# Relu written into the gated tile itself, a third result tile, and one load moved to GpSimd's queue

## The chip, the cores and the metric

The kernel runs on one core of one Trainium2 chip. The metric is the device time in microseconds of one execution. Every figure of a stage below is from the profile of one execution, whose span (2257.6 us) is a little under the device time. TensorE (PE) multiplies matrices, VectorE (DVE) and ScalarE (ACT) work element by element, GpSimd (POOL) does so too and can issue transfers, and SyncE (SP) issues most transfers.

## What is computed

A causal depthwise convolution with seven softmaxed taps per head runs over x (8 sequences of 4096 tokens, 192 channels). Its result, as 32768 rows of 192, goes through a two-layer net with a hard-swish gate:

```python
h = x @ w_in                       # 192 -> 2048
relu6 = np.clip(h + 3.0, 0.0, 6.0)
g = h * relu6 / 6.0
return (g @ w_out).astype(np.float32)   # 2048 -> 192
```

In the kernel the gate is `min(relu(h/6 + 0.5), 1) * h`, which is the same.

## The kernel before, in words

**Blocks.** The tokens are cut into 32 blocks of 1024 (`NB`), each as two halves of 512 that lie on two halves of the partitions. The order of all instructions is written out by hand; each engine takes its own in that order, and a queue issues its transfers in that order too.

**Block 0** is special: the weights are still being rounded and prepared, and its layers run in plain fp32. Its first layer goes through `h_out`, its second through `out_direct`. There four output parts at a time are multiplied into one PSUM bank, the bank is transposed by VectorE into a tile `xt` (L388), and `store_rows` issues four stores from that tile. Twelve parts make three such rounds, and the pool `ot` has two tiles `xt`. Between the matmuls and the transpose of the first round the job `prepare` (L758) is emitted: it splits w_in into three fp32r parts, runs block 1's convolution taps, makes the three parts of block 1's y (`halves_of_y`, each part followed by two transfers on SP's queue that swap its partition halves), and then loads block 2's x (L768), also on SP's queue. The stores of block 0 come after that in the queue.

**Blocks 1 to 31.** `first_layer` (L480) makes 16 chunks of h, each of two PSUM banks. `begin(n)` takes one of four slots of banks, multiplies the high parts and the low parts (12 matmuls, L492), and has ScalarE scale the banks by 4097 (L503). `end(n)` adds the mixed parts (6 matmuls), then ScalarE computes the Relu into a tile `r6` (L302), then VectorE gates it (L306) into `g`, and the slot is free for `begin(n + 4)`. `begin` runs two chunks ahead of `end`. Between the chunks there are jobs: the convolution taps of the block after (L731 on VectorE; the first tap, L729, on ScalarE). In block 1 that first tap is the job after chunk 1, since x of block 2 is still on its way; in later blocks it is emitted in the second layer of the block before. Chunks 0 to 7 use y as it lies (the OWN half), chunks 8 to 15 the swapped one.

`second_layer` (L534) does the products of the Strassen-like scheme (L342), with sums of the quarters of g by GpSimd, by an accumulating transfer (L530) and by VectorE, overwrites three quarters of g in place, and stores through `xt` (L453). The last block's final round is cut into two halves of tokens (L576).

**Tiles that matter here.** `g`, 64 KB per partition, is alive throughout. `r6` (pool `rs`) has two tiles of 4 KB, `xt` (pool `ot`) two of 2 KB, and x (pool `xs`) a single tile, so block 2's x can be loaded only when block 1's taps are done.

Of the kernel before, what the change touches and what calls it, by code (L numbers as in the profile page):

```python
# [8 lines left out]
ALU = mybir.AluOpType  # L9
ACT = mybir.ActivationFunctionType  # L10
AX = mybir.AxisListType
F32 = mybir.dt.float32
# [13 lines left out]
def kernel(  # L26
# [8 lines left out]
    nc = tc.nc  # L35
    P = nc.NUM_PARTITIONS
# [6 lines left out]
    N = 512  # L43
    G = 2
    TB = G * N
    D2 = P // 2
# [14 lines left out]
    cst = ctx.enter_context(tc.tile_pool(name="cst", bufs=1))  # L61
    xs = ctx.enter_context(tc.tile_pool(name="xs", bufs=1))
    ys = ctx.enter_context(tc.tile_pool(name="ys", bufs=1))
    rs = ctx.enter_context(tc.tile_pool(name="rs", bufs=2))
    ot = ctx.enter_context(tc.tile_pool(name="ot", bufs=2))
    ps = ctx.enter_context(tc.tile_pool(name="ps", bufs=1, space=bass.MemoryType.PSUM))
    start_pools, first_in = ExitStack(), ExitStack()
    stg = start_pools.enter_context(tc.tile_pool(name="stg", bufs=8))
# [3 lines left out]
    def x_source(i):  # L72
        b, t0 = i // BPB, (i % BPB) * TB
        src = xT[b].rearrange("(p s) t -> p s t", s=K3)
        head = PAD if t0 == 0 else 0
        return head, src[..., t0 - PAD + head : t0 + N], src[..., t0 + N - PAD : t0 + TB]

    def load_x(i):
        x = xs.tile([P, K3, PAD + N], F32, name="x")
        head, lower, upper = x_source(i)  # L80
        if head:
            nc.vector.memset(x[0:D2, :, 0:PAD], 0.0)
        nc.sync.dma_start(out=x[0:D2, :, head:], in_=lower)
        nc.sync.dma_start(out=x[D2:P, :, :], in_=upper)
        return x


# [1 line left out]
    for base, dma in ((0, nc.scalar), (D2, nc.sync)):  # L89
        dma.dma_start(  # L90
            out=w_sb[base : base + D2],
            in_=weight.unsqueeze(1).to_broadcast([H, GJ, KC]),
# [3 lines left out]
    x_tiles = {0: xs.tile([P, K3, PAD + N], F32, name="x")}  # L96
# [121 lines left out]
    for n in range(AHEAD):  # L218
# [8 lines left out]
        out=e_sb[:], in0=w_sb[:], in1=mx[:].to_broadcast([P, KC]), op=ALU.subtract  # L227
# [45 lines left out]
    g4 = g[:].rearrange("p c h k n -> p c (h k) n")  # L273
# [4 lines left out]
    psum = ps.tile([P, 2 * 4, N], F32, name="psum")  # L278
    free_banks = list(range(2 * 4))

    def take():
        return free_banks.pop(0)

    def give(b):
        free_banks.append(b)
# [15 lines left out]
    def relu(r6, h):  # L301
        nc.scalar.activation(r6, h, ACT.Relu, bias=half[:], scale=1.0 / 6.0)  # L302

    def gate(out, r6, h):

        nc.vector.scalar_tensor_tensor(  # L306
            out=out, in0=r6, scalar=1.0, in1=h, op0=ALU.min, op1=ALU.mult
        )

    def h_mm(c, group, bs, s, order=range(K3)):  # L310
# [4 lines left out]
    def g_of(c, group, k):  # L315

        return g[:, c, k, k if group == OWN else 1 - k]

    def h_out(c, group, bs, between):
        r6 = rs.tile([P, 2, N], F32, name="r6")  # L320
        for k, b in enumerate(bs):
            relu(r6[:, k], psum[:, b])
        between()
        for k, b in enumerate(bs):
            gate(g_of(c, group, k), r6[:, k], psum[:, b])
            give(b)


# [64 lines left out]
    def g_sums(engine, which, slots, width):  # L393

        forms = {
            3: (S3, A11, A21, ALU.subtract),
            2: (S2, S1, A11, ALU.subtract), 4: (S4, A12, S2, ALU.subtract),
        }
        for n in which:
            o, a, b, op = forms[n]  # L400
            for p in slots[::width]:
                r = slice(p, p + width)
                engine.tensor_tensor(out=o[:, r], in0=a[:, r], in1=b[:, r], op=op)  # L403
# [42 lines left out]
    def add(out, x, y, op=ALU.add):  # L446
        nc.vector.tensor_tensor(out=out, in0=x, in1=y, op=op)  # L447
# [13 lines left out]
    def r32(ap):  # L461
        return ap.bitcast(F32R)
# [9 lines left out]
    def w_parts(high, low, mix, w):  # L472
        high_of(high, w, EPS)
        from_high(mix, high, 4097.0, w, ALU.subtract)
        from_high(low, high, -4096.0, w, ALU.add)
        nc.scalar.mul(r32(mix), mix, -4096.0)
# [3 lines left out]
    def first_layer(i, jobs):  # L480

        slots = {}

        def both(n):
            return psum[:, 2 * slots[n] : 2 * slots[n] + 2]

        def mms(n, part, start=False, stop=False):
            group, c = divmod(n, NP)
            for s in range(K3):
                for k in range(2):  # L490
                    r = slice(k * D2, (k + 1) * D2)
                    nc.tensor.matmul(  # L492
                        out=psum[:, 2 * slots[n] + k], lhsT=r32(w_in_parts[part][r, c, s]),
                        rhs=r32(y_parts[part][r, group, s]),
                        start=start and s == 0, stop=stop and s == K3 - 1,
                        skip_group_check=True,
                    )

        def begin(n):
            slots[n] = free_slots.pop(0)  # L500
            mms(n, HIGH, start=True)
            mms(n, LOW)
            nc.scalar.mul(both(n), both(n), 4097.0)  # L503

        def end(n):
            group, c = divmod(n, NP)
            mms(n, MIX, stop=True)
            r6 = rs.tile([P, 2, N], F32, name="r6")
            relu(r6[:], both(n))
            gate(g4[:, c, 1:3] if group else g4[:, c, 0::3], r6[:], both(n))  # L510
            free_slots.append(slots[n])

        count = 2 * NP
        begin(0)
        begin(1)
        for job in jobs.get(-1, ()):
            job()
        for n in range(count):
            if n == count - 3:
                begin(n + 2)  # L520
            end(n)
            if n < count - 3:
                begin(n + 2)
            for job in jobs.get(n, ()):
                job()
            if n > NP and n % 2:
                pair = slice(n - NP - 1, n - NP + 1)
                g_sums(nc.gpsimd, (3,), range(NP)[pair], 2)
                if n + 1 < count:
                    nc.gpsimd.dma_start(out=S1[:, pair], in_=A22[:, pair], accum_op=ALU.add)  # L530
                else:
                    add(S1[:, pair], A21[:, pair], A22[:, pair])
# [77 lines left out]
    with tc.manual_schedule():  # L610
# [4 lines left out]
            out=c_sb[:], in0=e_sb[:], in1=sm[:].to_broadcast([P, KC]), op=ALU.mult  # L615
# [14 lines left out]
        b = take()  # L630
        for _ in range(3):

            nc.tensor.matmul(
                out=psum[:, b], lhsT=zeros[:, 0:P], rhs=zeros[:], start=True, stop=True
# [58 lines left out]
        n = 3  # L693
        for slot, (c, group) in enumerate(parts):
            first = slot < len(early)
            if first:
                bs = early[c, group]
            else:
                bs = take(), take()
                for s in range(K3):  # L700
                    h_mm(c, group, bs, s)
            more = slot in slots

            def between():
                if more:
                    join(n)
                    clamp(n + 1)

            if slot == 6:
                x_tiles[1] = load_x(1)  # L710
            h_out(c, group, bs, (lambda: None) if first else between)
            if more:
                split(n + 2)
                if first:
                    between()
                n += 1
# [10 lines left out]
        def conv_jobs(i):  # L727
            x = x_tiles.pop(i)
            jobs = [lambda: nc.scalar.mul(y[:], x[:, :, 0:N], c_sb[:, 0:1])]  # L729
            for k in range(1, KC):  # L730
                jobs.append(lambda k=k: nc.vector.scalar_tensor_tensor(  # L731
                    out=y[:], in0=x[:, :, k : k + N], scalar=c_sb[:, k : k + 1], in1=y[:],
                    op0=ALU.mult, op1=ALU.add,
                ))
            return jobs
# [17 lines left out]
        def halves_of_y():  # L753
            y_high()
            y_low()
            y_mix()

        def prepare():  # L758
            for n in range(0, NP, 4):
                r = slice(n, n + 4)  # L760
                w_parts(*[w[:, r] for w in w_in_parts], w_in[:, r])
            for job in conv_jobs(1):
                job()
            first_in.close()
            later = ctx.enter_context(tc.tile_pool(name="later", bufs=1, reuse_waits="tile"))
            y_parts.extend(later.tile([P, 2, K3, N], F32, name=f"y{n}") for n in range(3))
            halves_of_y()
            x_tiles[2] = load_x(2)  # L768

        out_direct(0, [prepare])  # L770
        w_sums(((T3, B22, B12),))
# [51 lines left out]
```

## Time and profile before

Three executions took 2260.67, 2260.86 and 2260.90 us. From the profile:

| engine | busy us | share |
|---|---|---|
| PE | 2243.0 | 99% |
| DVE | 1756.3 | 78% |
| ACT | 1316.1 | 58% |
| POOL | 492.2 | 22% |

| group | count | mean ns |
|---|---|---|
| first-layer matmul, L492, 64x512 | 8928 | 388 |
| second-layer matmul, L342, 128x512 | 9376 + 1488 | 590 |
| Relu, L302, 128x1024 | 528 | 1087 |
| gate, L306, 128x1024 | 528 | 1186 |
| scaling, L503, 128x1024 | 496 | 1009 |

A block from 1 on takes 69.1 us in the steady state: 32.9 in the first layer and 36.2 in the second. In the views, a line gives the line of the code, the engine, the operation, and the tiles it writes and reads; an arrow `A <- B` in the list of waits says that A's engine was idle until B was done. Matmuls overlap, so their busy times do not add up to elapsed time.

### The profile page before, as it was taken

How to read it: one execution, taken by the hardware profiler on the slowest of the kernel's cores; microseconds unless marked ns; L12 is line 12 of the kernel's file. 1: busy time of each engine (PE TensorE's matmuls, PEld its weight loads, DVE VectorE, ACT ScalarE, POOL GpSimd, SP SyncE). 2: the span in 40 equal slices, each digit the busy share in tenths (PEclk: the TensorE clock that was granted, in tenths of full speed). 3: DMA queues.
4: the chain of work that ended last, by engine and by line, in shares of the span. 5: the costliest groups of instructions: out<-in, count | busy, mean ns of one | idle time of the engine just before them, and what ended most of it. 6: DMA issues, size and time to landing. Idle time of an engine off the chain costs nothing.

```text
span 2257.6 us, 45592 instructions
## 1 busy us (share of the span) xinstructions
PE 2243.0 (99%) x20008; PEld 1212.5 (54%) x20008; DVE 1756.3 (78%) x1575; ACT 1316.1 (58%) x1428; POOL 492.2 (22%) x245
## 2 busy tenths in 40 slices
PE   9999999999999999999999999999999999999998
PEld 5355554555544555545555445554455554455544
DVE  8778877787877788777878777787778787787865
ACT  7366654566544666545665456665466654566643
POOL 2222102222012221122220222211222202222112
PEclk9999999999999999999999999999999999999999
DMA  6343345442354433454423544334544235443342
GB/s 154 68 92 69 54 87 99 92 87 53 67 99 95 92 63 57 90 99 90 85 53 71 99 94 94 57 63 90 99 89 83 52 75 99 94 93 55 61 79 43
DMA packets 262630, 182.52 MB, mean 81 GB/s; under 512 B 208992, under 2 KB 214112, under 8 KB 262432
## 3 DMA queue, kind: packets, MB, share of 16 engines
q1 hardware_dynamic: 236344, 130.39, 28.9%
q0 software_dynamic: 25392, 49.03, 12.5%
q8 instruction: 156, 2.56, 0.5%
q14 instruction: 42, 0.34, 0.1%
q10 hardware_dynamic: 696, 0.20, 0.0%
HBM read 31.72 MB, written 25.17 MB: 25 GB/s over the span
## 4 chain that ended last, share of the span: by engine, by line
PE 94%; DVE 3%; ACT 2%; DMA 1%; issue 0%; SPq 0%; ACTq 0%; DVEq 0%
PE psum L342 49%; PE psum L492 45%; ACT r L302 1%; DVE y L731 1%; DVE w_in L468 1%; DMA out_dram<-xt 0%; DVE y L255 0%; ACT scale L186 0%; DVE c L447 0%; ACT sig L183 0%; DMA x<-in_x_dram 0%; DVE g L306 0%; ACT sig L189 0%; DVE xt L453 0%; DVE top L175 0%
## 5 line engine op out<-in xcount | busy, mean ns | idle before, releaser
L342 PE MATMUL psum<-g,w_out 128*32 128x512 f32 (+1 forms) x9376 | 1165.4, 590 | 0.0
L492 PE MATMUL psum<-y,w_in 64*128 64x512 f32 x8928 | 1025.3, 388 | 5.6 <-DVE xt L388 5.6
L492 PEld LDWEIGHTS psum<-y,w_in 64*128 64x128 f32 x8928 | 830.4, 184 | 213.1 <-issue 26.0
L403 POOL TENSOR_TENSOR s<-g 128x1024 f32<-128x1024 f32 x124 | 376.8, 3039 | 1629.9 <-DVE g L306 1628.8
L306 DVE SCALAR_TENSOR_TENSOR g<-r,psum 128x1024 f32<-128x1024 f32 (+1 forms) x528 | 619.9, 1186 | 129.0 <-ACT r L302 125.2
L342 PEld LDWEIGHTS psum<-g,w_out 128*32 128x32 f32 x9376 | 339.9, 110 | 650.6 <-issue 638.8
L503 ACT ACTIVATE psum<-psum 128x1024 f32<-128x1024 f32 x496 | 500.4, 1009 | 266.7 <-PE psum L492 264.5
L302 ACT ACTIVATE r<-psum,half 128x1024 f32<-128x1024 f32 (+1 forms) x528 | 568.2, 1087 | 11.4 <-DVE g L306 10.6
L439 ACT COPY c<-psum 32x512 f32<-32x512 f32 x248 | 143.5, 579 | 516.4 <-PE psum L342 513.8
L731 DVE SCALAR_TENSOR_TENSOR y<-x,c_sb,y 128x1536 f32<-128x1536 f32 x186 | 337.2, 1813 | 0.2
L447 DVE TENSOR_TENSOR c<-c,psum 96x512 f32<-96x512 f32 (+2 forms) x251 | 170.7, 680 | 211.1 <-ACT c L439 182.7
L403 DVE TENSOR_TENSOR g<-g 128x2048 f32<-128x2048 f32 x124 | 276.8, 2272 | 0.0
L342 PE MATMUL psum<-s,w_out 128*32 128x512 f32 x1488 | 218.3, 592 | 0.0
L342 PEld LDWEIGHTS psum<-s,w_out 128*32 128x32 f32 x1488 | 61.2, 110 | 148.4 <-issue 148.4
L447 DVE TENSOR_TENSOR g<-g 128x1024 f32<-128x1024 f32 x31 | 38.0, 1225 | 124.5 <-POOL s L403 124.5
L530 POOL DMA_DIRECT2D g<-g x93 | 111.8, 1203 | 29.4 <-POOL s L403 29.4
L453 DVE STREAM_TRANSPOSE xt<-c 96x512 f32<-96x512 f32 (+4 forms) x157 | 109.7, 699 | 7.2 <-DMA out_dram<-xt 1.9
L447 DVE TENSOR_TENSOR c<-c,c 96x512 f32<-96x512 f32 (+1 forms) x124 | 84.8, 684 | 5.0 <-ACT c L439 1.8
L542 ACT COPY c<-psum 96x512 f32<-96x512 f32 x31 | 18.0, 582 | 101.3 <-PE psum L342 101.3
L744 DVE TENSOR_TENSOR y<-y,y 128x1536 fp32r<-128x1536 f32 x31 | 54.3, 1752 | 1.6 <-ACT y L465 1.6
L468 DVE SCALAR_TENSOR_TENSOR y<-y,y 128x1536 fp32r<-128x1536 f32 x31 | 54.3, 1752 | 0.0
L465 ACT ACTIVATE y<-y 128x1536 fp32r<-128x1536 f32 x31 | 45.8, 1478 | 12.0 <-DVE y L731 12.0
(51 smaller groups left out, 274.1 us busy)
## 6 DMA issues: line engine op xcount, KB each, us to landing
y<-y SPq DMA_DIRECT2D x186, 384.0 KB, 5.8
g<-g POOLq DMA_DIRECT2D x93, 512.0 KB, 5.3
out_dram<-xt SPq DMA_DIRECT2D x380, 64.0 KB, 2.0
x<-in_x_dram SPq DMA_DIRECT2D x55, 388.5 KB, 7.9
stage<-in_moe_w_in_dram SPq DMA_DIRECT2D x16, 192.0 KB, 4.6
stage<-in_moe_w_out_dram SPq DMA_DIRECT2D x8, 384.0 KB, 5.1
x<-in_x_dram SPq DMA_DIRECT2D x7, 384.0 KB, 8.3
y_swapped<-y SPq DMA_DIRECT2D x6, 128.0 KB, 2.4
```

Source lines behind the costliest of these rows:

```text
L302: nc.scalar.activation(r6, h, ACT.Relu, bias=half[:], scale=1.0 / 6.0)
L306: nc.vector.scalar_tensor_tensor(out=out, in0=r6, scalar=1.0, in1=h, op0=ALU.min, op1=ALU.mult)
L342: lambda p=p: nc.tensor.matmul(out=bank[j * QS : (j + 1) * QS, tokens], lhsT=w_out[:, p, w, cols], rhs=x[:, p, tokens], start=(first and p ...
L403: engine.tensor_tensor(out=o[:, r], in0=a[:, r], in1=b[:, r], op=op)
L439: nc.scalar.copy(out=dst[rows(q)], in_=src[rows(j)])
L447: nc.vector.tensor_tensor(out=out, in0=x, in1=y, op=op)
L453: nc.vector.transpose(out=xt[r, tokens], in_=c[r, tokens])
L468: nc.vector.scalar_tensor_tensor(out=r32(out), in0=high, scalar=scale, in1=x, op0=ALU.mult, op1=op)
L492: nc.tensor.matmul(out=psum[:, 2 * slots[n] + k], lhsT=r32(w_in_parts[part][r, c, s]), rhs=r32(y_parts[part][r, group, s]), start=start an ...
L503: nc.scalar.mul(both(n), both(n), 4097.0)
L530: nc.gpsimd.dma_start(out=S1[:, pair], in_=A22[:, pair], accum_op=ALU.add)
L731: jobs.append(lambda k=k: nc.vector.scalar_tensor_tensor(out=y[:], in0=x[:, :, k : k + N], scalar=c_sb[:, k : k + 1], in1=y[:], op0=ALU.mu ...
```

## The change

Relu writes its result into the place in `g` where the gated value will stand, and the gate works there in place. The pool of `r6` goes, and the room serves a third `xt`. Block 2's x is loaded by GpSimd's queue instead of SP's, where it stood ahead of block 0's stores. The first two edits belong together: dropping `r6` makes the room for the third result tile.

```diff
-    rs = ctx.enter_context(tc.tile_pool(name="rs", bufs=2))
-    ot = ctx.enter_context(tc.tile_pool(name="ot", bufs=2))
+    ot = ctx.enter_context(tc.tile_pool(name="ot", bufs=3))
...
-    def load_x(i):
+    def load_x(i, dma=nc.sync):
...
-        nc.sync.dma_start(out=x[0:D2, :, head:], in_=lower)
-        nc.sync.dma_start(out=x[D2:P, :, :], in_=upper)
+        dma.dma_start(out=x[0:D2, :, head:], in_=lower)
+        dma.dma_start(out=x[D2:P, :, :], in_=upper)
...
-    def gate(out, r6, h):
+    def gate(g_, h):
...
-            out=out, in0=r6, scalar=1.0, in1=h, op0=ALU.min, op1=ALU.mult
+            out=g_, in0=g_, scalar=1.0, in1=h, op0=ALU.min, op1=ALU.mult
...
-        r6 = rs.tile([P, 2, N], F32, name="r6")
         for k, b in enumerate(bs):
-            relu(r6[:, k], psum[:, b])
+            relu(g_of(c, group, k), psum[:, b])
         between()
         for k, b in enumerate(bs):
-            gate(g_of(c, group, k), r6[:, k], psum[:, b])
+            gate(g_of(c, group, k), psum[:, b])
...
-            r6 = rs.tile([P, 2, N], F32, name="r6")
-            relu(r6[:], both(n))
-            gate(g4[:, c, 1:3] if group else g4[:, c, 0::3], r6[:], both(n))
+            to = g4[:, c, 1:3] if group else g4[:, c, 0::3]
+            relu(to, both(n))
+            gate(to, both(n))
...
-            x_tiles[2] = load_x(2)
+            x_tiles[2] = load_x(2, nc.gpsimd)
```

## The prediction

> **What bounds the kernel now.** I read the page first: engine shares, then the chain of work that ended last.
>
> ```profile
> PE 2243.0 (99%) x20008; PEld 1212.5 (54%) x20008; DVE 1756.3 (78%) x1575; ACT 1316.1 (58%) x1428; POOL 492.2 (22%) x245
> PE psum L342 49%; PE psum L492 45%; ACT r L302 1%; DVE y L731 1%; DVE w_in L468 1%; DMA out_dram<-xt 0%; DVE y L255 0%; ACT scale L186 0%; DVE c L447 0%; ACT sig L183 0%; DMA x<-in_x_dram 0%; DVE g L306 0%; ACT sig L189 0%; DVE xt L453 0%;
> ```
>
> TensorE is the bound, and 94% of the chain is its two matmul lines. So an edit is worth what it takes out of TensorE's few gaps, or out of the end after its last matmul. I looked for those gaps in the list of waits, cut to 99.9 to 141.1 us, where block 1's first layer runs:
>
> ```profile
> DVE xt L388 <- DMA out_dram<-xt: 14.4, 1, 14.4
> PE psum L492 <- DVE xt L388: 5.6, 1, 5.6
> PEld psum L492 <- ACT psum L503: 0.7, 3, 0.4
> PEld psum L492 <- DVE g L306: 0.5, 1, 0.5
> ```
>
> The columns are microseconds, times, longest. Block 0's third transpose waits 14.4 us for a store to land, and TensorE waits 5.6 us for that transpose. What the gap costs is in the table of windows (length; busy time of PE, PEld, DVE, ACT, POOL; granted clock; DMA share; GB/s):
>
> ```profile
> 99.93:105.70 5.77, 5.77 (x52) 4.46 (x48) 0.00 (x0) 3.68 (x4) 1.16 (x1) 1.00 1.00 204
> 105.70:111.25 5.55, 0.00 (x0) 0.00 (x0) 0.77 (x2) 1.39 (x2) 0.00 (x0) 0.72 0.93 146
> 111.25:115.00 3.75, 3.75 (x18) 2.96 (x20) 2.19 (x2) 0.78 (x1) 0.00 (x0) 0.50 0.45 70
> 177.36:210.28 32.92, 32.92 (x292) 26.75 (x296) 29.14 (x24) 30.44 (x31) 7.69 (x3) 1.00 0.16 25
> ```
>
> Block 2's first layer, the same 288 matmuls, takes 32.92 us, 0.1143 us each. Block 1's runs from 99.93 to 141.10, 41.17 us. The excess of 8.25 us splits up: 5.55 idle; 3.75 us at clock 0.50, of which half, 1.87, is lost; then the later waits for ACT and DVE, 0.36 and 0.49. The sum is 8.27. Why the store is late is in the timeline of SP's queue:
>
> ```profile
> 97.23 1.57 SPq L267 DMA_DIRECT2D y<-y  x1
> 98.85 1.41 SPq L83 DMA_DIRECT2D x<-in_x_dram  x1
> 100.30 1.42 SPq L84 DMA_DIRECT2D x<-in_x_dram  x1
> 101.81 11.36 SPq L361 DMA_DIRECT2D out_dram<-xt  x12
> ```
>
> Six swaps of y and the two loads of block 2's x stand ahead of the first store, though the first two transposes were done at 96.1. The third needs the first one's tile. VectorE idles from 96.1 to 110.5, and the gates of chunks 0 and 1 stand behind it.
>
> **What the Trainium skill says.** "TensorE: Matmul & The Clock Gate", section "What's actually happening": the clock falls to half after an idle window of about 3.4 us, and needs a busy one to come back. The trace agrees: 0.50 after the 5.55 us gap, until 115.0. So the gap is worth more than its idle time. "DMA: Bandwidth & Descriptors", section "Issuing engines are not separate DMA queues": transfers from all queues share the same 16 DMA engines; another queue saves only issue time. The trace has DMA share 1.00 from 99.93 to 105.70, so moving x creates no bandwidth. "SBUF — State Buffer", section "SBUF: two separate sides": descriptors of a transfer issued by GpSimd can be held up by some VectorE instructions. Here GpSimd's own issues (L530) take 1.20 us, and their 512 KB land in 5.3 us, beside a busy VectorE, so I see no large penalty.
>
> **The change part by part.**
>
> *Third result tile.* Block 0 has three transposes and now three tiles, so L388 waits for no store. Its matmuls start their last at about 99.9; with its 0.7 us the transpose is done near 101.1. The chunk that needs its bank starts at TensorE after 48 matmuls, at 105.7. So the 5.55 us of idle go, and the half clock with them: 1.87. Together 7.42.
>
> *What comes back.* In block 1 one ScalarE job (L729, the first tap of block 2's y) stands in the first layer, after chunk 3's scaling; in later blocks it lies in the second layer. Today it runs at 115.15, while TensorE creeps. After the change it meets TensorE at full speed. ScalarE takes 1.94 us for a chunk's scaling and Relu back to back (L503 starts at 117.61, 119.55, 121.49); TensorE gives it 18 x 0.1143 = 2.06. A job of 1.47 us start to start is thus 12 chunks of slack. Worked forward from 99.93: chunk 3's high and low parts end after 60 matmuls and two short waits, near 106.9; its scaling starts at 107.2, L729 at 108.1, chunk 2's Relu at 109.6 and chunk 4's scaling at 110.6, done 111.6. TensorE wants that at 111.0: a wait of 0.6. The Relus, and so the gates behind them, are late too, and chunk 8 waits for chunk 4's gate, about 0.4 (today 0.49 on the same kind of wait). Each restart costs 0.1 in the trace. That is 1.2 in place of today's 0.85. Block 1's first layer becomes 32.92 + 1.2 = 34.1, against 41.17: **7.05 saved**.
>
> *x by GpSimd's queue.* GpSimd is free from 77.2 to 99.25 (L212 waits for PE 22.0 us). The load can issue once the last tap of block 1 is done, at 89.9, ahead of the swaps. Its two issues at 1.2 each and 8.5 us to landing (today's for the same transfer) put it at about 101. Swaps share the engines, but today swaps and x together are through at 108.8, having begun at 91.5; sharing evenly, x should be in by 104. L729 wants it at 108.1. Left on SP it would land at 100.30 + 8.5 = 108.8 and cost 0.7. I count the move as keeping that 0.7 away. The swapped halves are first read by chunk 8, at about 117, so a few microseconds of delay hide. The stores behind have no reader in block 0.
>
> *Relu into g, gate in place.* It pays for the tile: two r6 tiles of 4 KB go, one xt of 2 KB comes. Same instruction counts, 528 Relus and 528 gates. Relu now carries the wait for g's earlier readers. Those are TensorE's products of the block before, which are ahead of this chunk's matmuls in TensorE's own order, so Relu's wait for its bank already covers them; the GpSimd sums, the accumulating transfers and VectorE's sums were done tens of microseconds earlier. What queues behind a late Relu is the next scaling, and TensorE waits for that. Duration: L302 takes 1.11 for 1024 elements into r6 and I expect the same into g, whose runs are 512 long. An in-place gate has a neighbour in L731, in place at 1.81 us for 1536, the gate's 1.22 per 1024 in rate. The wait for r6 (10.6 us in 31 waits of 0.3) goes, but it falls when TensorE is already in the second layer: nothing.
>
> *Blocks 2 to 31.* Their first layers show no gap beyond 0.3 us, so nothing is gained there.
>
> *The end.* The last transposes wait once more for a store:
>
> ```profile
> 2252.36 0.43 DVE L453 STREAM_TRANSPOSE xt<-c 32x256 f32<-32x256 f32 x1 [0.63 <-DMA out_dram<-xt]
> ```
>
> From here VectorE runs to the end at 2255.1 and the last store follows. With three tiles the 0.63 goes. SP's issues are close behind, so I take 0.45.
>
> Sum: 7.05 + 0.45 = 7.5. 2260.86 - 7.5 = **2253.4 us**.
>
> **Rivals.**
> - *A larger gain.* L729's delay finds slack that I miss, and the full 8.25 + 0.63 goes: 2252.0. For it: today's waits after the restart were just 0.85. Against it: ScalarE has 0.12 per chunk.
> - *A wait takes the place of the one removed.* x comes late, by contention or slow descriptors, and ScalarE, with all Relus behind it, stands at L729. Landing at 111 costs 2.5 to 3 more: 2256.2. Against it: 18 us between its issue and its use.
> - *Hidden anyway.* The transpose still waits, for something else in VectorE's or SP's order: 2260.9. Against it: the wait names the store alone, and its time matches the landing.
> - *Slower.* ScalarE and VectorE have 0.12 and about 0.05 us of slack per chunk. If Relu or gate in g takes 0.17 longer, by access pattern or added semaphores, ScalarE sets the pace at 0.05 over TensorE's, 16 chunks in 31 blocks: 25 us, less the gain, 2278. For it: the slack is really that thin. Against it: nothing in the trace shows writes into strided g slower; the gate wrote there already.
>
> **How the numbers follow.** Forecast 0.70; larger gain 0.09; late x 0.09; hidden 0.06; slower 0.06. Faster by over 0.2% means below 2256.3: the first three, 0.88. Same: 0.06. Slower: 0.06. The range takes in forecast, larger gain and late x: 2251.8 to 2256.3.
>
> **What would show it.** Right: the wait of L388 for a store is gone; no clock of 0.50 near 111 us; block 1's first layer takes 33 to 35 us, with a ScalarE wait of some 0.6 near 111; later blocks stay at 69.1 us; the end is shorter by some 0.5. Wrong: ScalarE waiting for x at L729; L302 above 1.2 us; a first layer of later blocks above 33.

## The result, and the profile after

The changed kernel takes 2253.56 us (median of 6, 2253.05 to 2253.59) against 2260.78 us for the kernel before (median of 6, 2260.64 to 2261.09): 7.22 us less, a ratio of 0.9967 with a 95% interval of 0.9955 to 0.998. The forecast was 2253.4, in a range of 2251.8 to 2256.3. In the code of the changed kernel the lines have moved by one or two: L386 is the transpose of block 0 (L388 before), L490 the first layer's matmul, L501 the scaling, L301 the Relu, L305 the gate, L727 and L729 the convolution taps.

The page of the changed kernel, engines and the chain by line:

```profile
PE 2242.8 (100%) x20008; PEld 1213.1 (54%) x20008; DVE 1755.1 (78%) x1575; ACT 1313.6 (58%) x1428; POOL 493.9 (22%) x247
PE 98%; DVE 1%; ACT 0%; DMA 0%; issue 0%; SPq 0%; ACTq 0%; DVEq 0%
```

TensorE's busy time is the same within 0.2 us, and its share of the chain has gone from 94% to 98%: what went was waiting. The list of waits of the changed kernel, cut to 95 to 140 us (engine and line, what it waited for, microseconds, times, longest):

```profile
DVE xt L386 <- PE psum L340: 4.1, 1, 4.1
PEld psum L490 <- ACT psum L501: 1.0, 2, 0.8
PEld psum L490 <- DVE g L305: 0.5, 1, 0.5
PE psum L490 <- ACT psum L501: 0.4, 1, 0.4
```

The third transpose waits only for its own matmuls, and TensorE no longer waits for it. In place of the 5.6 us stand a wait for ScalarE's scaling and one for a gate. The table of windows shows what that is worth (length; busy time of PE, PEld, DVE, ACT, POOL; granted clock; DMA share; GB/s). The first two windows are those shown of before; the last three are block 1's first layer, block 2's, and everything from the last block's second layer on:

```profile
105.70:111.25 5.55, 5.31 (x48) 4.06 (x44) 2.42 (x3) 5.54 (x6) 0.00 (x0) 1.00 0.80 123
111.25:115.00 3.75, 3.57 (x32) 2.96 (x34) 3.03 (x3) 3.75 (x5) 0.00 (x0) 1.00 0.33 52
99.78:133.84 34.06, 33.55 (x292) 26.64 (x288) 24.52 (x19) 31.52 (x32) 8.86 (x4) 1.00 0.42 77
170.03:203.01 32.98, 32.98 (x292) 26.78 (x288) 29.18 (x24) 30.43 (x31) 7.70 (x3) 1.00 0.15 25
2208.82:2251.70 42.88, 36.30 (x402) 12.92 (x400) 26.06 (x30) 7.27 (x12) 5.99 (x3) 0.97 0.27 44
```

Where TensorE did nothing for 5.55 us it now issues 48 matmuls, and the clock stays at 1.00 where it was 0.50. For the same stages in the kernel before:

```profile
99.93:141.10 41.17, 35.55 (x293) 27.90 (x289) 24.34 (x19) 31.50 (x32) 8.85 (x4) 0.92 0.37 65
177.29:210.21 32.92, 32.92 (x293) 26.75 (x289) 29.14 (x24) 30.37 (x31) 7.69 (x3) 1.00 0.15 25
2214.30:2257.64 43.34, 36.29 (x402) 12.89 (x400) 26.15 (x30) 7.40 (x12) 6.01 (x3) 0.97 0.26 44
```

Block 1's first layer is shorter by 41.17 - 34.06 = 7.11 us, and the end by 43.34 - 42.88 = 0.46. All second layers take 36.19 in both. The later first layers are longer, 32.98 against 32.92: over 30 blocks the trace sums to 989.4 against 987.6, 1.8 us. With 0.15 from an earlier start of block 1's stage this gives 7.11 + 0.46 + 0.15 - 1.8 = 5.9, the difference of the two spans (2257.6 and 2251.7). The difference of the medians is larger, 7.2. Experiments 3 to 6 below show that the 1.8 us are no part of the change. A second profile of each kernel (experiments 5 and 7) gives 41.24 - 34.06 = 7.18 in block 1's first layer and 43.34 - 42.86 = 0.48 at the end, less 0.17 in the later first layers: 7.5 in span. The saving is thus 7.2 to 7.5 us.

The timeline of GpSimd's queue in the changed kernel, where x is loaded, and of SP's:

```profile
90.27 0.66 POOL L82 DMA_DIRECT2D x<-in_x_dram  x1 [13.28 <-DVE y L729]
90.92 0.64 POOL L83 DMA_DIRECT2D x<-in_x_dram  x1
...
97.02 0.93 SPq L266 DMA_DIRECT2D y<-y  x1
98.04 13.65 SPq L359 DMA_DIRECT2D out_dram<-xt  x12
```

The load is issued as soon as block 1's taps release the tile, 8.6 us earlier than before, and its two halves land at 95.2 and 96.9. The stores start at 98.0 instead of 101.8. At the end, the transpose that waited 0.63 us for a store no longer does:

```profile
2246.29 0.44 DVE L451 STREAM_TRANSPOSE xt<-c 32x256 f32<-32x256 f32 x1
```

### The profile page after: what moved, and what is told of

Same layout as the page of the kernel before. It is cut to its first block, busy times and chain, and to the rows that moved or that the text cites. A ratio compares the mean times of both kernels' runs of the same rounds, so it can differ in the third digit from the quotient of the medians.

```text
span 2251.7 us, 46078 instructions
## 1 busy us (share of the span) xinstructions
PE 2242.8 (100%) x20008; PEld 1213.1 (54%) x20008; DVE 1755.1 (78%) x1575; ACT 1313.6 (58%) x1428; POOL 493.9 (22%) x247
## 4 chain that ended last, share of the span: by engine, by line
PE 98%; DVE 1%; ACT 0%; DMA 0%; issue 0%; SPq 0%; ACTq 0%; DVEq 0%
PE psum L340 51%; PE psum L490 45%; PE psum L295 2%; DVE c L445 0%; DMA x<-in_x_dram 0%; DVE xt L451 0%; DVE y L729 0%; DMA out_dram<-xt 0%; ACT y L727 0%; ACT g L301 0%; SPq L100 0%; SPq L132 0%; DVE g L305 0%; DVE top L174 0%; PE psum L623 0%
## 5 line engine op out<-in xcount | busy, mean ns | idle before, releaser
L490 PE MATMUL psum<-y,w_in 64*128 64x512 f32 x8928 | 1025.1, 388 | 0.5 <-ACT psum L501 0.4
L490 PEld LDWEIGHTS psum<-y,w_in 64*128 64x128 f32 x8928 | 830.0, 184 | 207.9 <-issue 26.0
L305 DVE SCALAR_TENSOR_TENSOR g<-g,psum 128x1024 f32<-128x1024 f32 (+1 forms) x528 | 618.6, 1186 | 129.8 <-ACT g L301 129.4
L501 ACT ACTIVATE psum<-psum 128x1024 f32<-128x1024 f32 x496 | 500.3, 1009 | 259.6 <-PE psum L490 257.6
L301 ACT ACTIVATE g<-psum,half 128x1024 f32<-128x1024 f32 (+1 forms) x528 | 565.0, 1088 | 0.8
L729 DVE SCALAR_TENSOR_TENSOR y<-x,c_sb,y 128x1536 f32<-128x1536 f32 x186 | 337.0, 1812 | 0.2
```

The costliest lines, as they stand in the source:

```text
L305: nc.vector.scalar_tensor_tensor(out=g_, in0=g_, scalar=1.0, in1=h, op0=ALU.min, op1=ALU.mult)
L490: nc.tensor.matmul(out=psum[:, 2 * slots[n] + k], lhsT=r32(w_in_parts[part][r, c, s]), rhs=r32(y_parts[part][r, group, s]), start=start an ...
L729: jobs.append(lambda k=k: nc.vector.scalar_tensor_tensor(out=y[:], in0=x[:, :, k : k + N], scalar=c_sb[:, k : k + 1], in1=y[:], op0=ALU.mu ...
```

## Experiments

The theory: block 0's third transpose made the gap because it reused a tile whose stores had not landed; the gap cost its idle time and a stretch of half clock. The main rival: SP's queue order made it, so that moving x was the edit that counted. A second question is what Relu in g costs or brings, a third what is left in block 1.

### 1. The third tile alone

```diff
@@ out_direct, kernel before
-            xt = ot.tile([P, N], F32, name="xt")
-            nc.vector.transpose(out=xt[:], in_=bank)
+            with ExitStack() as own:
+                pool = ot
+                if r == 8:
+                    pool = own.enter_context(tc.tile_pool(name="ot0", bufs=1, reuse_waits="tile"))
+                xt = pool.tile([P, N], F32, name="xt")
+                nc.vector.transpose(out=xt[:], in_=bank)
...
```

The release of the bank and the stores follow inside the `with`. The pool is open for the third round only (`r == 8`), when room that block 1 will use is still free, so r6 can stay.

> The kernel before, with one edit: block 0's third transpose writes into a tile of its own, from a pool opened only there. r6 stays, x stays on SP's queue, ot keeps two tiles. My theory (the reused tile made the gap): no wait of L388 for a store, no half clock, block 1's first layer 34.1 plus 0.7 for x landing at 108.8 = 34.8 us against 41.2; later first layers 32.92 as before; the end as before. About 2254.4 us. Rival (SP's queue order made the gap, and x had to leave it): the gap stays, first layer 41.2, 2260.8 us.

Measured: 2254.51 us (2254.34 to 2254.65), ratio 0.9971 (0.996 to 0.9982). The third transpose waits for its matmuls only, block 1's first layer took 34.69 us, and the clock stayed at 1.00 (a line of the list of waits, then the window of that stage):

```profile
DVE xt L392 <- PE psum L342: 4.1, 1, 4.1
99.62:134.31 34.69, 33.57 (x292) 26.60 (x288) 24.54 (x19) 31.61 (x32) 8.84 (x4) 1.00 0.44 77
```

ScalarE's timeline shows the wait for x that the move was to keep away:

```profile
106.81 1.01 ACT L507 ACTIVATE psum<-psum 128x1024 f32<-128x1024 f32 x1
108.33 1.58 ACT L733 ACTIVATE y<-x,c_sb 128x1536 f32<-128x1536 f32 x1 [0.51 <-DMA x<-in_x_dram]
```

The tile alone brings 41.17 - 34.69 = 6.5 of the 7.1 us. The rival falls.

### 2. The move of x alone

```diff
@@ prepare, kernel before (load_x takes the queue as an argument)
-            x_tiles[2] = load_x(2)
+            x_tiles[2] = load_x(2, nc.gpsimd)
```

> The kernel before, with one edit: block 2's x by GpSimd's queue. Two result tiles, r6 kept. My theory: the 16 DMA engines are the limit, x's bytes still come before the stores, so the first round's stores land near 109 instead of 110.2 and the third transpose starts near 109; the gap shrinks by 1 to 1.5 us only, the clock still falls to half. First layer near 39.8, about 2259.5 us. Rival (queue order): stores land early, at 102 to 104, no gap left, first layer near 34, about 2253.6 us.

Measured: 2260.3 us (2259.92 to 2260.92), ratio 0.9997 (0.9989 to 1.0006): by time not told from before. In the list of waits:

```profile
DVE xt L388 <- DMA out_dram<-xt: 13.3, 1, 13.3
PEld psum L492 <- DVE xt L388: 4.8, 1, 4.8
PE psum L492 <- DVE xt L388: 4.4, 1, 4.4
```

The stores are issued 3.7 us earlier (98.08 against 101.81), yet the transpose starts only 1.3 us earlier (109.16 against 110.48). That fits the theory: the DMA engines are full with x and the swaps (DMA share 1.04 from 99.7 to 105.5), so earlier issue alone does not bring the stores in. The gap is 4.4 us instead of 5.6, and the clock falls to 0.50 all the same:

```profile
109.50:112.00 2.50, 2.07 (x10) 1.70 (x12) 2.50 (x3) 0.00 (x0) 0.00 (x0) 0.50 0.56 84
```

The first layer takes 40.33, so the rival falls. Alone, the move takes 41.17 - 40.33 = 0.84 us off that stage. With the tile there it takes off 0.56: the kernel with tile and move (next but one) has 34.13 against 34.69, and 2254.26 us against 2254.51.

### 3. Relu into g alone

```diff
@@ changed kernel
-    ot = ctx.enter_context(tc.tile_pool(name="ot", bufs=3))
+    ot = ctx.enter_context(tc.tile_pool(name="ot", bufs=2))
-            x_tiles[2] = load_x(2, nc.gpsimd)
+            x_tiles[2] = load_x(2)
```

> The changed kernel with the other two edits undone: Relu into g and the gate in place, but two result tiles and x on SP's queue. My theory: block 1's gap is all there (first layer 41.2); the later 30 first layers take 32.98 instead of 32.92, as in the changed kernel, so this edit by itself costs 30 x 0.06 = 1.8 us: the span is 2259.4. Rival (the 0.06 per block comes from the third tile or from shifted semaphores of the transfers): later first layers 32.92, span 2257.6.

Measured: 2260.87 us (2260.57 to 2261.06), ratio 0.9999 (0.9991 to 1.0008). The gap is there as before, 5.9 us:

```profile
DVE xt L386 <- DMA out_dram<-xt: 14.4, 1, 14.4
PEld psum L490 <- DVE xt L386: 6.3, 1, 6.3
PE psum L490 <- DVE xt L386: 5.9, 1, 5.9
```

Block 1's first layer took 41.57, the later ones 32.98, the span 2259.3: close to the numbers of my theory. But by time this kernel is not slower than before (2260.87 against 2260.95), so the 0.06 per block is not a cost of the edit. The next run says so more plainly.

### 4. Tile and move, r6 kept

The edits of experiments 1 and 2 together, on the kernel before.

> The kernel before with the third tile for block 0 from a pool of its own and x by GpSimd's queue; r6 kept, so Relu doesn't write g. My theory: block 1's first layer 34.1 as in the changed kernel, later first layers 32.92, the end as before (43.35 from the last second layer's start). Span 2257.6 - 7.1 - 0.1 = 2250.4, that is 1.3 us under the changed kernel: Relu into g is only the price of the room. Rival (Relu into g helps block 1): first layer over 34.5, time not under the changed kernel's 2253.6.

Measured: 2254.26 us (2254.13 to 2254.47), ratio 0.997 (0.9959 to 0.9982), span 2252.4. My theory missed by 2 us: r6 is there, and the later first layers take 32.98 all the same. Block 1's first layer took 34.13, near the changed kernel's 34.06, so Relu in g does not help block 1 either. The windows of block 1's and block 2's first layer:

```profile
99.77:133.91 34.14, 33.65 (x293) 26.60 (x289) 24.55 (x19) 31.52 (x32) 8.85 (x4) 1.00 0.42 78
170.09:203.07 32.98, 32.98 (x292) 26.75 (x288) 29.17 (x24) 30.42 (x31) 7.68 (x3) 1.00 0.15 25
```

The end, 43.47 from the last second layer's start, is as long as before; in the changed kernel it is 42.88, because there the third tile serves the last block too. So what writing Relu into g brings is room for a third tile throughout, worth 0.5 to 0.6 us at the end. For block 0 the two edits need not go together, as a tile that lives for one round is enough there. No run tried a third tile throughout beside r6.

### 5. The kernel before once more

> The kernel before, unchanged, profiled once more. All of the kernels profiled so far take 32.98 us for the later first layers, whether Relu writes g or r6; the first profile of before has 32.92, and its execution took 2259.45 us where before takes 2260.9 otherwise. If that first profile was only an uncommonly quick execution: later first layers 32.98, time near 2260.9, span near 2259.1, block 1's first layer again 41.2. If before really has shorter first layers: 32.92 again, and all three edits would cost 0.06 per block alike, which I think unlikely.

Measured: 2260.52 us, span 2258.7. The later first layers of this execution sum to 988.8, between the 987.6 of the first profile and the 989.4 of most experiments; block 1's took 41.24. In the second profile of the changed kernel (experiment 7) they vary from block to block, between 32.92 and 32.98. Two kernels of experiment 6, with 17 and 10 transposes, hold all three edits and have 32.92 in every later block (sum 987.6). So a block's first layer varies between these values from execution to execution, whatever the edits, and the first profile of before was a quick one, 2259.45 us where the six executions of the result took 2260.6 to 2261.1. What decides was not found.

### 6. The gap made longer and shorter

In the changed kernel the third transpose is done several times over into the same tile, which keeps its bank busy without any wait for a transfer. The 3.4 us in the expectations are the window that the prediction cites. Each kernel was profiled in a single execution, so only the stages are compared.

```diff
@@ out_direct, changed kernel; 12, 17 and 10 times
-            nc.vector.transpose(out=xt[:], in_=bank)
+            for _ in range(12 if r == 8 else 1):
+                nc.vector.transpose(out=xt[:], in_=bank)
```

> The changed kernel, with block 0's third transpose done 12 times over, so that its bank comes free near 107.7 instead of 100.6: a made gap of some 2.2 us at TensorE, shorter than one idle window of the clock. My theory (a gap over some 3.4 us halves the clock, a shorter one doesn't): clock 1.00 throughout, block 1's first layer 34.06 + 2.2 = 36.3. Rival (any gap here brings the half clock, or the half clock in before came from something else, as the transfers): a stretch of 0.50, 37.5 or more.

> The same with 17 transposes: the bank comes free near 111, a gap of 5.4 us as in before, but with no wait for a store. My theory: the clock falls to 0.50 for one stretch until about 115, block 1's first layer 41.1, as in before. Rival (the length of the gap alone matters): clock 1.00, 34.06 + 5.4 = 39.5.

> The changed kernel with block 0's third transpose done 10 times over. A transpose took 0.75 us in the run with 12, not 0.65, so that gap was 3.3 us and the clock did fall; this one is some 1.9 us and ends near 107.4, before 108, where the stretches of half clock began. If a gap must be over some 2.5 us before that point to bring the half clock: clock 1.00 throughout, block 1's first layer 34.06 + 1.9 = 35.9. If any gap of this kind brings it: 0.50 for 6.8 us again, some 38.0.

A transpose took 0.75 us here, not 0.65, so the first two gaps came out longer than planned: 3.3 and 7.1 us. The third was 1.9.

| repeated | gap at TensorE, us | clock 0.50 from, us | for, us | block 1's first layer, us |
|---|---|---|---|---|
| 1 (changed kernel) | 0 | never | | 34.06 |
| 10 | 1.9 | never | | 36.27 |
| 12 | 3.3 | 108.1 | 6.83 | 39.44 |
| 17 | 7.1 | 109.4 | 6.83 | 42.76 |

The windows with 12 and with 10 transposes, the granted clock third from the end:

```profile
105.50:107.70 2.20, 0.00 (x0) 0.00 (x0) 2.10 (x4) 1.36 (x2) 0.00 (x0) 1.00 0.93 141
110.00:113.00 3.00, 3.00 (x18) 2.31 (x16) 1.00 (x1) 1.21 (x2) 0.00 (x0) 0.50 0.60 91
```

```profile
105.50:107.50 2.00, 0.14 (x4) 0.05 (x2) 1.93 (x4) 1.49 (x2) 0.00 (x0) 1.00 1.05 166
107.50:111.00 3.50, 3.50 (x30) 2.87 (x32) 2.14 (x2) 1.83 (x2) 0.00 (x0) 1.00 0.68 102
```

A gap of 1.9 us costs 36.27 - 34.06 = 2.2, about itself. One of 3.3 costs 5.4: itself, plus half of what remains of the slow stretch from 108.8 to 114.9 (3.1), less about 1.0 of the waits for ScalarE and the gate, of which that run's list has only 0.3 left. A gap without any wait for a transfer brings the half clock, so the half clock of the kernel before came from the gap. The theory's point, that such a gap costs more than itself, holds; the length that I named for it was too large, as 3.3 us were enough. But these runs do not show that length alone decides. With 12 transposes TensorE was idle when the clock fell, at 108.1, 102.4 us after its first rise. With 10 the gap had closed at 107.5, and that same point would have come at 109.5. The last section takes this up.

### 7. What is left in block 1

```diff
@@ before first_layer(i, jobs), changed kernel
             if i == 1:
-                jobs = {n + 2: job for n, job in jobs.items()}
-                jobs[1] = conv[:1]
+                conv[0]()
             first_layer(i, jobs)
```

> The changed kernel, with block 2's first tap on ScalarE emitted before block 1's first layer instead of after chunk 1, and the other taps two chunks earlier, as in later blocks. My theory (this job alone makes what is left of block 1's excess): x lands near 97, ScalarE is idle until 101.5, so the tap runs at 97 to 98.6 for nothing; block 1's first layer 32.98 instead of 34.06; 2253.56 - 1.08 = 2252.5 us. Rival (the excess comes from the cold start of the stage or from the transfers under way, DMA share 1.0): the first layer stays at 33.8 or more, 2253.3 us or more.

Measured: 2250.69 us (2250.58 to 2252.08), where before took 2259.2 on the same chip; ratio 0.9961 (0.9948 to 0.9975). The first layer took 32.92, so the rival falls. But six of the nine executions of before took 2259.0 to 2259.4 there and three 2260.9 to 2261.3. The two levels are about as far apart as 30 blocks of 0.06 us, and both occur on this one chip, though the next expectation speaks of a difference from chip to chip. So this version was measured again beside the changed kernel.

> The changed kernel, unchanged, beside the next run on one chip, since before and the experiments differ by up to 1.8 us from chip to chip. Block 1's first layer 34.06; 2252 to 2253.6 us.

> The changed kernel with block 2's first tap ahead of block 1's first layer, as measured already, now on one chip with the changed kernel. Block 1's first layer 32.95 against 34.06, so 1.1 us under the changed kernel's time on the same chip. If the earlier difference of 2.9 us was real in whole: 2.9 under.

Measured on one chip: 2253.21 us (2253.09 to 2253.26) for the changed kernel and 2251.94 us (2251.57 to 2252.05) with the early tap, 1.27 less; the first layer 34.06 and 32.95. ScalarE's timeline of the kernel with the early tap:

```profile
89.62 1.49 ACT L463 ACTIVATE y<-y 128x1536 fp32r<-128x1536 f32 x1 [11.43 <-DVE y L729]
97.37 1.57 ACT L727 ACTIVATE y<-x,c_sb 128x1536 f32<-128x1536 f32 x1 [6.27 <-DMA x<-in_x_dram]
101.42 1.01 ACT L501 ACTIVATE psum<-psum 128x1024 f32<-128x1024 f32 x1 [2.47 <-PE psum L490]
```

The tap runs in a hole where ScalarE has nothing else, and the job is what block 1's first layer had left over the later ones: 1.11 us of the stage. On this chip this version takes less time than both kernels; its ratio to before is 0.9962 (0.9947 to 0.9977).

## Why the prediction was right

- **The gap and the half clock, 5.55 + 1.87.** Right in both parts, by the windows after and by experiments 1 and 6. That the tile, and not the queue, was the cause is shown by experiments 1 and 2. One reading was loose: the half clock did not begin after a gap of 5.55 us but inside it, at 108.2, 2.5 us in, which is why the window of the gap has a mean clock of 0.72. The cost was taken from the part after 111.25 and so came out right. The transpose was done at 100.6 and not 101.1; TensorE needed the bank only at 105.7.
- **What comes back, 1.2 us.** Block 1's first layer came out at 34.06, forecast 34.1. The place was right too. ScalarE in the changed kernel:

```profile
107.89 1.57 ACT L727 ACTIVATE y<-x,c_sb 128x1536 f32<-128x1536 f32 x1
109.36 1.11 ACT L301 ACTIVATE g<-psum,half 128x1024 f32<-128x1024 f32 x1
110.36 1.03 ACT L501 ACTIVATE psum<-psum 128x1024 f32<-128x1024 f32 x1
```

  The job was forecast at 108.1, the Relu behind it at 109.6, the scaling at 110.6; all three came 0.2 earlier. The wait for the scaling is 0.8 at TensorE's weight loads and 0.4 at its matmuls, where 0.6 was forecast; the wait for the gate is 0.5 (0.4). That this job makes the excess is shown by experiment 7.
- **x by GpSimd's queue, 0.7 kept away.** Measured 0.56 (34.69 against 34.13). x landed at 96.9, not at 101: the estimate of 8.5 us to landing was SP's, behind the swaps; here the load was ahead of them and its halves landed in 4.9 and 6.0. The swaps landed later, a median of 9.9 us after issue instead of 6.6, but nothing reads them until chunk 8. None of this reached the sum.
- **Relu into g, nothing.** Durations are unchanged (Relu 1088 ns against 1087, gate 1186 against 1186), and experiment 3 gives no time. I had left the slack per chunk as the ground for the slower rival; nothing used it.
- **The end, 0.45.** Measured 0.46.
- **Later blocks, nothing.** Right, though it took three runs to see it: the trace shows 0.06 per block more, and I took that for a cost of Relu in g in the expectations of experiments 3 and 4. It was the level of single executions. The forecast was anchored to the median of the times and so did not suffer. That the total came within 0.2 us is in part luck: levels 1.8 us apart occur on one chip (experiment 7), and the executions of the two kernels seem to have lain at like levels by chance.
- **Not foreseen:** the small differences before block 1 (99.93 against 99.78). They vary among all kernels profiled, 99.4 to 99.9, and are not part of the change.

Of the rivals, the larger gain failed for the reason given against it (ScalarE's 0.12 us per chunk), but experiment 7 shows that it could be had by moving one job.

## What to carry to other kernels

A bound engine at 99% still had a gap of 5.6 us worth 7.1 us: look at the one place where a tile is reused before its store has landed, and at what else sits in the same queue ahead of that store. A job that costs nothing while an engine is starved costs something once the gap in front of it is closed, so work out where it lands afterwards, and move it into an idle stretch if there is one. And compare stages over more than one profile before a difference of some hundredths per block is given a cause.

## What the runs showed of the hardware that was not expected

- The Trainium skill, "TensorE: Matmul & The Clock Gate", section "What's actually happening", gives an idle window of about 3.4 us. Here less idle time was enough: the half clock began 2.5 us (kernel before) and 2.6 us (experiment 6, 12 transposes) into the gap. It lasted 6.83 us each time, although TensorE was busy again from 111.3 and 108.8. In the clock records of all 13 profiles every fall comes a whole number of steps of 3.413 us after the first rise to full clock: 30 steps (102.4 us) in the six with a fall in block 1, and 656 to 659 at the end of every run. On that grid, the step just before the fall held 2.5 to 3.4 us of idle in those six (kernel before: the step from 104.76 to 108.17, idle from 105.70). With 10 transposes no step held more than 1.3 (the step from 106.13 to 109.54, idle until 107.45). So the runs fit a window of 3.41 us on a fixed grid in which enough idle time must lie, and then the place of a gap counts as well as its length. The same gap at another place on the grid was not tried.
- SP's issue of a swap of y took 0.5 to 0.6 us for the first three and 1.6 us for the next three (kernel before, from 93.9 us on); in the changed kernel the six took 0.5 to 1.7. A queue that is issued in order can thus get later by more than the number of its transfers suggests. Full DMA engines alone do not explain it: the DMA share was already 1.09 from 92.6 to 93.9, where the third swap took 0.64 us, and of the stores that followed, 64 KB each, the first three took 0.5 to 0.6 with a share of 0.98 and the next two 2.3 and 2.4. The cause stays open.
